# Interleaving two output-projection units, re-cutting the weight slices and splitting the last batch's loads in a fused attention and SwiGLU kernel

## The chip, the cores and the metric

The kernel runs on one core of one Trainium2 chip. The metric is device time in microseconds (us), the median of several executions. The kernel before was put beside every run, so that both are taken on the same chip.

## The reference, cut to what matters

```
# attention with softmaxed features: q over the head dim, k over the sequence
q_s = softmax(q, axis=-1);  k_s = softmax(k, axis=2)          # (8, 8, 576, 64)
kv  = einsum('bhsd,bhse->bhde', k_s, v)
x   = einsum('bhsd,bhde->bhse', q_s, kv)                      # -> 4608 tokens x 512
# SwiGLU block
out = (silu(x @ w_gate) * (x @ w_val)) @ w_out                # 512 -> 1536 -> 512
```

## The kernel before: the parts that matter

Weights are cast to bf16 by DMAs that GpSimd issues. The gate and value weights come in slices of columns, the output weights in four slices of three row blocks. The loads of batch 1 are issued by SyncE when the first output-weight slice has landed.

```python
for c0, n in ((0, 128), (128, 128), (256, 256), (512, 256), (768, 384), (1152, 384)):
    w_slice(wg, moe_w_gate, c0, n)
    w_slice(wv, moe_w_val, c0, n)
w_dma = [wo_slice(m0, 3) for m0 in (0, 3, 6, 9)]
...
after = w_dma[0]
for what, src in (("q", q), ("v", v), ("k", k)):        # batch 1
    ...load(what, src, 1, G, ..., after=after)
```

Batch 0 goes through twelve column blocks (m) of gate and value matmuls. Then come output units 0 and 1 (128 tokens each), and between them and the next ones the attention of batch 1:

```python
for m in range(MT):                       # MT = 12
    m_unit(0, S, m, by_group=(m == 0))    # 8 gate + 8 value matmuls, silu, product
exp_of("q", 1, 0); exp_of("q", 1, 1)      # ScalarE
norm_sum(1, 0); norm_mul(1, 0); norm_sum(1, 1)   # VectorE
o_out(0, o_mm(0), nc.scalar)              # 12 matmuls over the output weights
o_out(1, o_mm(1), nc.scalar)
p2 = o_mm(2, m1=4)
turn_pe(1, 0, 0); turn_pe(1, 0, 1)        # TensorE transposes of VectorE's product
...
i = norm_mul(1, 1)                        # VectorE, second product
cast_v(1, 0)                              # GpSimd
...
o_mm(2, p2, m0=4)
turn_pe(1, 1, 0); turn_pe(1, 1, 1)
...                                       # keys and values, then x of batch 1
chunks = [(S, 448)] + ...                 # "chunk 1" below is the first of these
```

The tail of the program stores the last unit in two parts, each half through SyncE and half through ScalarE (`o_last`).

The softmax here doesn't subtract the row's maximum and nothing guards it: scores larger than these inputs give would overflow.

Of the kernel before, what the change touches and what calls it, by code (L numbers as in the profile page):

```python
# [15 lines left out]
def kernel(  # L16
# [10 lines left out]
    nc = tc.nc  # L27

    B, H, S, D = q.shape
# [3 lines left out]
    MT = d_ff // 128  # L33
    T = S // 64
# [3 lines left out]
    BANKS = ((0, 5), (5, T))  # L38
# [8 lines left out]
    def bank(name):  # L47
        return psp.tile([128, 512], FP32, tag="ps", name=name)
# [16 lines left out]
    def head_ap(src, b, G, t0=0, t1=T):  # L65
        return bass.AP(
            tensor=src.tensor,
            offset=src[b, 4 * G].offset + 64 * t0,
            ap=[[T * 64, 128], [2 * HSTR, 2], [1, (t1 - t0) * 64]],
        )  # L70

    def load(what, src, b, G, pieces=((0, T),), after=None):
        t_ = ld.tile([128, 2, T * 64], FP32, tag=what, name=what)
        raw[what, b, G] = t_
        last = None
        for t0, t1 in pieces:
            last = nc.sync.dma_start(out=t_[:, :, 64 * t0:64 * t1], in_=head_ap(src, b, G, t0, t1))
            if after is not None:
                tc.add_manual_dep(last.ins, after.ins.name, SYNC, reason="order of loads")
                after = None  # L80
        return last

    def load_kv(b):
        for G in range(NG):
            load("k", k, b, G)
            load("v", v, b, G)

    def w_slice(dst, src, c0, n):
        ap = bass.AP(
            tensor=src.tensor,  # L90
            offset=src[0, c0].offset,
            ap=[[d_ff, 128], [128 * d_ff, KT], [1, n]],
        )
        return nc.gpsimd.dma_start(out=dst[:, :, c0:c0 + n], in_=ap)  # L94
# [9 lines left out]
    def copy(eng, out, in_):  # L104
        if eng is nc.scalar:
            nc.scalar.copy(out=out, in_=in_)
        else:
            eng.tensor_copy(out=out, in_=in_)  # L108
# [18 lines left out]
    def norm_sum(b, G, pieces=((0, T),)):  # L127
        s = st[b, G]
        eq2 = s["eq"].rearrange("p t h d -> p (t h) d")
        rs = at.tile([128, 2 * T], FP32, tag="rs", name="rs")  # L130
        first = None
        for t0, t1 in pieces:
            i = nc.vector.reduce_sum(  # L133
                out=rs[:, 2 * t0:2 * t1], in_=eq2[:, 2 * t0:2 * t1, :], axis=mybir.AxisListType.X
            )
            first = first or i
        rr = s["rr"] = at.tile([128, 2 * T], FP32, tag="rr", name="rr")
        nc.vector.reciprocal(out=rr, in_=rs)
        return first
# [152 lines left out]
    def store(j, o_sb, c0=0, c1=512, engs=(nc.sync, nc.sync)):  # L292
        for half in range(2):
            b, t = divmod(2 * j + half, T)
            dst = bass.AP(
                tensor=out.tensor,
                offset=out[b * S + t, c0].offset,
                ap=[[T * d_model, 64], [1, c1 - c0]],
            )
            engs[half].dma_start(out=dst, in_=o_sb[64 * half:64 * half + 64, c0:c1])  # L300

    def o_mm(j, o_ps=None, m0=0, m1=MT):
        if o_ps is None:
            o_ps = bank("o_ps")
        r0 = (j * 128) % RING
        for m in range(m0, m1):
            nc.tensor.matmul(  # L307
                out=o_ps, lhsT=hr[:, m, r0:r0 + 128], rhs=wo[:, m, :],
                start=(m == 0), stop=(m == MT - 1),
            )  # L310
        return o_ps

    def o_out(j, o_ps, eng=nc.vector):
        o_sb = osb.tile([128, 512], FP32, tag="o_sb", name="o_sb")
        copy(eng, o_sb, o_ps)
        store(j, o_sb)
# [20 lines left out]
    with tc.manual_schedule():  # L337
# [23 lines left out]
        norm_mul(0, 0, BANKS)  # L361
        norm_sum(0, 1, BANKS)

        for c0, n in ((0, 128), (128, 128), (256, 256), (512, 256), (768, 384), (1152, 384)):
            w_slice(wg, moe_w_gate, c0, n)
            w_slice(wv, moe_w_val, c0, n)
        w_dma = [wo_slice(m0, 3) for m0 in (0, 3, 6, 9)]
# [88 lines left out]
        norm_sum(1, 0)  # L456
        norm_mul(1, 0)
        norm_sum(1, 1)
        o_out(0, o_mm(0), nc.scalar)
        o_out(1, o_mm(1), nc.scalar)  # L460
        p2 = o_mm(2, m1=4)
        turn_pe(1, 0, 0)
        turn_pe(1, 0, 1)
# [35 lines left out]
        for ci, (c0, n) in enumerate(chunks):  # L499
            b = ci + 2  # L500
# [4 lines left out]
            for m in range(MT):  # L505
# [36 lines left out]
                if m == 8 and more:  # L542
                    for G in range(NG):
                        load("q", q, b + 1, G)
                    if b + 2 < B:
                        load_kv(b + 2)
# [4 lines left out]
        last = n_tok // 128 - 4  # L551
# [33 lines left out]
```

## Time and profile before

| what | value | read in |
|---|---|---|
| time, median of the first 3 runs | 312.39 us | runs |
| time of the one profiled execution | 313.74 us | runs |
| span of that execution | 311.6 us | page |
| TensorE busy / idle | 301.8 / 9.8 us | page, part 1 |
| first gate matmul | 14.21 us | TensorE's timeline |
| first output matmul | 38.76 us | TensorE's timeline |
| chunk 1 starts | 52.65 us | TensorE's timeline |
| last matmul to end of span | 4.09 us | trace |

In a timeline row the columns are start, duration, engine, source line, operation, output and inputs with their shape, the number of instructions merged, and in brackets the idle time before it with what ended it. ScalarE's timeline:

```profile
38.60 1.28 ACT L119 ACT_TABLE_LOAD   x1
40.48 1.16 ACT L119 ACTIVATE eq<-q 128x1152 bf16<-128x1152 f32 x1 [0.60 <-DMA q<-in_q_dram]
```

### The profile page before, as it was taken

How to read it: one execution, taken by the hardware profiler on the slowest of the kernel's cores; microseconds unless marked ns; L12 is line 12 of the kernel's file. 1: busy time of each engine (PE TensorE's matmuls, PEld its weight loads, DVE VectorE, ACT ScalarE, POOL GpSimd, SP SyncE). 2: the span in 40 equal slices, each digit the busy share in tenths (PEclk: the TensorE clock that was granted, in tenths of full speed). 3: DMA queues.
4: the chain of work that ended last, by engine and by line, in shares of the span. 5: the costliest groups of instructions: out<-in, count | busy, mean ns of one | idle time of the engine just before them, and what ended most of it. 6: DMA issues, size and time to landing. Idle time of an engine off the chain costs nothing.

```text
span 311.6 us, 5449 instructions
## 1 busy us (share of the span) xinstructions
PE 301.8 (97%) x2182; PEld 149.2 (48%) x2182; DVE 160.7 (52%) x274; ACT 146.1 (47%) x214; POOL 32.8 (11%) x39
## 2 busy tenths in 40 slices
PE   6899999999999999999999999999999999999994
PEld 2567744555444444444444444444444444444442
DVE  3834477946763567355836492639353334333321
ACT  5843468794764465547364637455143113312300
POOL 2950021510200110002000200000000000000000
PEclk9999999999999999999999999999999999999999
DMA  7999999989356906491729253605310302020034
GB/s 270 188 190 204 274 384 367 364 191 377 107 103 149 374 14 135 91 391 45 143 63 352 109 111 68 187 1 105 68 39 0 69 11 56 2 68 13 21 69 103
DMA packets 41690, 45.78 MB, mean 147 GB/s; under 512 B 18496, under 2 KB 25664, under 8 KB 41664
## 3 DMA queue, kind: packets, MB, share of 16 engines
q1 hardware_dynamic: 32752, 39.99, 43.2%
q0 software_dynamic: 8752, 5.31, 12.0%
q8 instruction: 17, 0.28, 0.4%
q10 hardware_dynamic: 160, 0.13, 0.1%
q14 instruction: 9, 0.07, 0.1%
HBM read 37.75 MB, written 9.44 MB: 151 GB/s over the span
## 4 chain that ended last, share of the span: by engine, by line
PE 85%; DMA 10%; POOL 2%; issue 0%; ACT 0%; SPq 0%; DVE 0%
PE o_ps L307 28%; PE g_ps L282 26%; PE u_ps L282 26%; DMA wo<-in_moe_w_out_dram 6%; DMA wv<-in_moe_w_val_dram 3%; PE kv L187 2%; DMA k<-in_k_dram 2%; PE xp L243 1%; POOL wg L94 1%; PE o_ps L327 1%; POOL wv L94 1%; POOL v L345 0%; PE tp L162 0%; POOL v L342 0%; ACT xt L257 0%
## 5 line engine op out<-in xcount | busy, mean ns | idle before, releaser
L289 ACT ACTIVATE sg<-g_ps 128x512 bf16<-128x512 f32 (+2 forms) x120 | 64.7, 554 | 134.6 <-PE g_ps L282 132.8
L290 DVE TENSOR_TENSOR hr<-sg,u_ps 128x512 bf16<-128x512 bf16 (+2 forms) x120 | 74.2, 630 | 88.3 <-PE u_ps L282 82.6
L282 PE MATMUL g_ps<-xt,wg 128*128 128x512 bf16 (+2 forms) x480 | 111.4, 358 | 0.4 <-DMA wg<-in_moe_w_gate_dram 0.3
L282 PE MATMUL u_ps<-xt,wv 128*128 128x512 bf16 (+2 forms) x480 | 111.3, 358 | 0.2 <-DMA wv<-in_moe_w_val_dram 0.2
L307 PE MATMUL o_ps<-wo,hr 128*128 128x512 bf16 x420 | 94.1, 379 | 0.5 <-DMA wo<-in_moe_w_out_dram 0.5
L282 PEld LDWEIGHTS <-wv 128*128 128x128 bf16 x480 | 46.9, 98 | 46.9 <-DMA wv<-in_moe_w_val_dram 0.5
L282 PEld LDWEIGHTS <-wg 128*128 128x128 bf16 x480 | 46.1, 98 | 46.2 <-DMA wg<-in_moe_w_gate_dram 0.8
L307 PEld LDWEIGHTS <-hr 128*128 128x128 bf16 x420 | 41.0, 98 | 49.3 <-issue 0.8
L108 DVE COPY o_sb<-o_ps 128x512 f32<-128x512 f32 x33 | 22.4, 680 | 39.2 <-PE o_ps L307 39.2
L122 POOL CAST vb<-v 128x1152 bf16<-128x1152 f32 x14 | 17.8, 1276 | 135.3 <-DMA v<-in_v_dram 90.7
L133 DVE TENSOR_REDUCE rs<-eq 128x18 f32<-128x1152 bf16 (+2 forms) x18 | 21.7, 1215 | 13.6 <-ACT eq L119 13.6
L147 DVE TENSOR_TENSOR qs<-eq,rr 128x1152 bf16<-128x1152 bf16 (+2 forms) x18 | 21.7, 1216 | 0.1
L119 ACT ACTIVATE eq<-q 128x1152 bf16<-128x1152 f32 (+2 forms) x18 | 18.3, 1051 | 5.3 <-DMA q<-in_q_dram 5.2
L119 ACT ACTIVATE ek<-k 128x1152 bf16<-128x1152 f32 (+2 forms) x17 | 17.9, 1101 | 0.5 <-DMA k<-in_k_dram 0.5
L289 ACT ACT_TABLE_LOAD x12 | 15.4, 1283 | 0.2
L119 ACT ACT_TABLE_LOAD x11 | 14.1, 1283 | 0.2
L257 ACT CAST xt<-xp 128x512 bf16<-128x512 f32 x14 | 7.8, 587 | 4.3 <-PE xp L243 4.3
L258 DVE CAST xt<-xp 128x512 bf16<-128x512 f32 x14 | 9.0, 683 | 0.7 <-PE xp L243 0.7
L372 PE MATMUL idle<-zero 128*128 128x512 bf16 x20 | 6.3, 465 | 3.0 <-DVE rs L133 1.8
L187 PEld LDWEIGHTS <-ek 64*64 64x64 bf16 x504 | 6.3, 107 | 1.7 <-ACT ek L119 0.4
L187 PE MATMUL kv<-vb,ek 64*64 64x65 bf16 x504 | 6.7, 194 | 0.0
L243 PE MATMUL xp<-qt,kn 64*64 64x512 bf16 (+1 forms) x112 | 6.7, 292 | 0.0
(43 smaller groups left out, 62.2 us busy)
## 6 DMA issues: line engine op xcount, KB each, us to landing
q<-in_q_dram SPq DMA_DIRECT2D x16, 576.0 KB, 8.6
out_dram<-o_sb SPq DMA_DIRECT2D x70, 128.0 KB, 2.3
k<-in_k_dram SPq DMA_DIRECT2D x15, 576.0 KB, 7.5
v<-in_v_dram SPq DMA_DIRECT2D x14, 576.0 KB, 8.7
wo<-in_moe_w_out_dram POOLq DMA_DIRECT2D x4, 384.0 KB, 15.3
wg<-in_moe_w_gate_dram POOLq DMA_DIRECT2D x2, 384.0 KB, 11.4
wv<-in_moe_w_val_dram POOLq DMA_DIRECT2D x2, 384.0 KB, 13.2
wg<-in_moe_w_gate_dram POOLq DMA_DIRECT2D x2, 256.0 KB, 7.7
```

Of the source, the lines that this page charges most:

```text
L108: eng.tensor_copy(out=out, in_=in_)
L119: nc.scalar.activation(out=e[:, t0:t1], in_=src[:, t0:t1], func=AF.Exp)
L122: return nc.gpsimd.tensor_copy(out=vbs[G][:, :, :, 0:64], in_=raw["v", b, G].rearrange("p h (t d) -> p t h d", d=64),)
L133: i = nc.vector.reduce_sum(out=rs[:, 2 * t0:2 * t1], in_=eq2[:, 2 * t0:2 * t1, :], axis=mybir.AxisListType.X)
L147: last = eng.tensor_mul(qs[:, t0:t1, :].rearrange("p t (h d) -> p (t h) d", d=64), eq2[:, 2 * t0:2 * t1, :], s["rr"][:, 2 * t0:2 * t1].to_ ...
L187: nc.tensor.matmul(out=kv[g][HALF[h], c:c + 65], lhsT=ek[HALF[g], t, h, :], rhs=vbs[G][HALF[g], t, h, :], start=(t == 0), stop=(t == T - 1),)
L243: nc.tensor.matmul(out=o[h][HALF[g], c:c + 64 * (t1 - t0)], lhsT=kn[HALF[h], g, G, :], rhs=qt[G][HALF[h], t0:t1, 64 * g:64 * g + 64], star ...
L258: nc.vector.tensor_copy(out=xt[:, 2 * G + 1, c0:c0 + 512], in_=main[G][1])
L282: nc.tensor.matmul(out=gu[a][i][:, 0:w_], lhsT=(wg, wv)[a][:, kk, ms], rhs=xt[:, kk, c:c + w_], start=(kk == 0), stop=(kk == KT - 1),)
L289: nc.scalar.activation(out=sg[:, 0:w_], in_=g_ps[:, 0:w_], func=AF.Silu)
L290: nc.vector.tensor_mul(hr[:, m, r:r + w_], sg[:, 0:w_], u_ps[:, 0:w_])
L307: nc.tensor.matmul(out=o_ps, lhsT=hr[:, m, r0:r0 + 128], rhs=wo[:, m, :], start=(m == 0), stop=(m == MT - 1),)
```

## The change

The intent is plain in the two waits that TensorE's timeline shows. Smaller slices bring the third column block sooner. Interleaving units 0 and 1 asks for the last output-weight slice after 18 matmuls and not after 9. The last batch's loads are cut in pieces: in the first hunk T is 9, and BANKS is the pair of ranges (0, 5) and (5, 9), so that a split load is two transfers.

```diff
     def load_kv(b):
+        whole = ((0, T),)
+        last = b == B - 1
         for G in range(NG):
-            load("k", k, b, G)
-            load("v", v, b, G)
+            load("k", k, b, G, BANKS if last else whole)
+            load("v", v, b, G, BANKS if last and G == 0 else whole)
@@
-        for c0, n in ((0, 128), (128, 128), (256, 256), (512, 256), (768, 384), (1152, 384)):
+        for c0, n in ((0, 128), (128, 128), (256, 128), (384, 256), (640, 384), (1024, 512)):
@@
-        o_out(0, o_mm(0), nc.scalar)
-        o_out(1, o_mm(1), nc.scalar)
+        p = [None, None]
+        for m0 in range(0, MT, 3):
+            for j in range(2):
+                p[j] = o_mm(j, p[j], m0, m0 + 3)
+        for j in range(2):
+            o_out(j, p[j], nc.scalar)
         p2 = o_mm(2, m1=4)
```

## The prediction

> **What bounds the kernel now.** I read the page first, then the list of what TensorE waited for, then the timelines of TensorE, ScalarE and VectorE over the first 55 us, then the landing times of the weight loads, and last the stretches table with the DMA rate. The page's first part says that TensorE is the bound of the whole:
>
> ```profile
> PE 301.8 (97%) x2182; PEld 149.2 (48%) x2182; DVE 160.7 (52%) x274; ACT 146.1 (47%) x214; POOL 32.8 (11%) x39
> ```
>
> Of the span of 311.6 us TensorE is idle for 9.8 us, and the view of its waits says where the named part of that lies:
>
> ```profile
> PE idle L372 <- DVE rs L133: 1.8, 1, 1.8
> PE idle L372 <- DVE sel L351: 1.2, 1, 1.2
> PE kv L395 <- DMA v<-in_v_dram: 0.9, 1, 0.9
> PE o_ps L307 <- DMA wo<-in_moe_w_out_dram: 0.5, 1, 0.5
> PE xp L200 <- DVE kn L408: 0.4, 1, 0.4
> PE g_ps L282 <- DMA wg<-in_moe_w_gate_dram: 0.3, 1, 0.3
> PE u_ps L282 <- DMA wv<-in_moe_w_val_dram: 0.2, 1, 0.2
> ```
>
> Only the three lines that name weights (0.5 + 0.3 + 0.2) can be touched by this change, since the others come before the first gate matmul at 14.2 us. After 53 us the list has no wait: the last 258 us are matmuls end to end. So what can be won or lost lies between 14.2 and 52.7 us, and TensorE's timeline shows the two waits that the change aims at, in brackets:
>
> ```profile
> 18.74 1.15 PE L282 MATMUL g_ps<-xt,wg 128*128 128x320 bf16 x8
> 20.13 1.16 PE L282 MATMUL u_ps<-xt,wv 128*128 128x320 bf16 x8 [0.23 <-DMA wv<-in_moe_w_val_dram]
> ...
> 41.41 0.81 PE L307 MATMUL o_ps<-wo,hr 128*128 128x512 bf16 x3 [0.54 <-DMA wo<-in_moe_w_out_dram]
> ```
>
> The steady step of eight such matmuls is 0.98 us (21.12, 22.10, 23.08 and so on), so the value matmuls of column block m=2 were due at 18.74 + 0.98 = 19.72 and started at 20.13: 0.41 us lost. The second line is output unit 0 at weight row block 9, which waits for the last quarter of the output weights.
>
> The reader should not stop there. Over the same stretch VectorE has a chain of its own (timeline of VectorE):
>
> ```profile
> 41.68 1.35 DVE L133 TENSOR_REDUCE rs<-eq 128x18 f32<-128x1152 bf16 x1 [1.94 <-ACT eq L119]
> 43.06 0.27 DVE L138 RECIPROCAL rr<-rs 128x18 f32<-128x18 f32 x1
> 43.37 1.36 DVE L147 TENSOR_TENSOR qs<-eq,rr 128x1152 bf16<-128x1152 bf16 x1
> 44.64 1.35 DVE L133 TENSOR_REDUCE rs<-eq 128x18 f32<-128x1152 bf16 x1
> 46.02 0.27 DVE L138 RECIPROCAL rr<-rs 128x18 f32<-128x18 f32 x1
> 46.32 1.36 DVE L147 TENSOR_TENSOR qs<-eq,rr 128x1152 bf16<-128x1152 bf16 x1
> ```
>
> It has no gap from 41.68 to 47.68. It starts when ScalarE has exponentiated the queries of batch 1, at 40.48, and ScalarE itself waited 0.60 us there for the load of q. TensorE needs its product at 47.74 for the transposes:
>
> ```profile
> 46.01 1.89 PE L307 MATMUL o_ps<-wo,hr 128*128 128x512 bf16 x8
> 47.74 0.68 PE L162 MATMUL tp<-ident,qs 128*128 128x128 bf16 x9
> ```
>
> 47.68 against 47.74: the two chains meet within 0.06 us. TensorE can't pass this point earlier, whatever it saves before it, unless q lands earlier. And q is issued only when the first output-weight slice has landed (the queue of SyncE waits 30.8 us for it, to 33.56). That slice comes after all gate and value slices in the same queue. So behind TensorE's 97% the stretch from 33.6 to 52.7 us is set by DMA.
>
> **What the Trainium skill says.** (1) "DMA: Bandwidth & Descriptors", section "Why small descriptors are slow (HBM only)": each packet has a fixed overhead, so short runs move fewer bytes per second. A slice of 128 columns is read in runs of 512 B and written, as bf16, in runs of 256 B. The trace agrees, in the stretches table (last number: GB/s of bytes written). The first row is mostly 128-column slices, the second mostly 256 and 384:
>
> ```profile
> 13.00:18.00 5.00, 4.24 (x79) 3.00 (x68) 2.78 (x8) 3.90 (x9) 4.17 (x7) 1.00 1.47 164
> 18.00:33.00 15.00, 14.77 (x120) 11.40 (x119) 5.74 (x14) 5.46 (x16) 3.48 (x5) 1.00 1.32 203
> ```
>
> (2) The same page, section "Issuing engines are not separate DMA queues": all queues end on the same 16 engines. The trace agrees: the last output-weight slice took 18.4 us to land against 14.6, 15.0 and 15.7 of the other three, as q, v and k of batch 1 came in beside it. (3) "Perfetto Trace Analysis", section "DMA Optimizations": splitting may let work start sooner if the DMA engines are generally idle. Here they are not between 2 and 60 us. (4) "TensorE: Matmul & The Clock Gate", section "Wait — 56ns, not 53.3ns?" gives 215.7 ns from start to start for 512 columns; the chain of waits has 24 output matmuls in 5.18 us, 215.8 each. It agrees, and I use the trace's.
>
> **The change part by part.** The count of instructions stays the same on TensorE, VectorE, ScalarE and GpSimd; SyncE gets three load issues more.
>
> *Slices of 3x128, 256, 384, 512 in place of 2x128, 2x256, 2x384.* Bytes and count stay, the sizes change. A 128-column slice is 0.131 MB written. Time by the two rates: before 4 x 0.131/0.164 + (4 x 0.262 + 4 x 0.393)/0.203 = 3.2 + 12.9 = 16.1 us; after 6 x 0.131/0.164 + 2 x (0.262 + 0.393 + 0.524)/0.203 = 4.8 + 11.6 = 16.4 us. So the whole column of weights, and with it q, comes some 0.3 us later. The third value slice landed at 20.05 (issue at 12.35, 7.7 to landing); with half its pair's bytes it comes about 2 x 0.262/0.203 - 2 x 0.131/0.164 = 1.0 us sooner, at 19.1, before it is due at 19.72: the wait of 0.41 goes. But slices get larger and are needed at their first column block. Due times of the value half, 1.96 us per block: m=3 at 21.7, m=5 at 25.6, m=8 at 31.5. Landings: 19.1 + 2.6 = 21.7; + 3.9 = 25.6; and for the last the measured 31.6 (17.66 + 13.9) plus 0.3 = 31.9. Two just on time and the last 0.4 late. Moreover the second-last value slice of before (15.28 + 12.5 = 27.8) landed 3.1 us after its partner, 1.2 more than its bytes need; if such a straggler hits the 384 slice now, m=5 waits 1.1. So 0.41 is taken out and 0.4 to 1.1 put back: a net of 0 to -0.7 us, about nothing. The first output matmul starts at 38.7 to 39.4 (before 38.76).
>
> *Units 0 and 1 interleaved.* The same 24 matmuls; the last slice is wanted after 18 of them and not after 9, 18 x 0.216 = 3.9 us after the start, at 42.6 or later, against a landing at 41.4 (23.00 + 18.4) to 41.7. The wait of 0.54 goes for certain. The evacuations of both units move together to about 44 us on ScalarE, which has 0.78 us idle before the second one: free.
>
> *What becomes of the saved time.* With 24 + 4 matmuls (6.05 us) TensorE reaches the transposes of batch 1 at 44.8 to 45.5. The first product is done at 43.37 + 1.36 = 44.73, plus 0.3 = 45.0. Then 0.5 of transposes and 1.73 of eight matmuls: 47.3 to 47.7; the second product is ready at 47.68 + 0.3 = 48.0. TensorE waits, and goes on at 48.0 where it was 47.74. The saved 0.54 becomes a wait on VectorE, and the later DMA costs about 0.25. From there to 52.65 the steps follow without slack (exponent of k done at 49.26, kv at 49.64, x at 51.56), so this passes to the end.
>
> *Last batch's keys and values in pieces.* Three more issues of about 0.5 us on SyncE at 163.7 to 165.9, with its next store only at 180.3; the exponents of these keys run at 189.0 and still wait for whole tiles. Hidden: 0.
>
> Sum: 0 + 0 + 0.25 + 0 = +0.25 us, from 312.39 to 312.6. As the rate of the small slices in the first row is partly the values' own loads, I take half: 312.5.
>
> **Rivals.** *TensorE gets both waits back* (0.41 + 0.54 = 0.95 us, to 311.4): it needs q to land about 1 us earlier. For it: landing times depend on the slowest of 16 engines, and the straggler of 1.2 us might vanish. Against: bytes and queue order ahead of q are the same. *The 512-column slice stalls* m=8 for over 1 us and exceeds what the later wait on VectorE hides (about 0.6): 313.3. For it: 31.9 against 31.5 is tight, and it is the largest of all; against: the interleaving gives slack behind it. *The pieces disturb the stores or the queue late*: against it, 14 us of idle SyncE after them and no wait of TensorE on a store anywhere.
>
> **Range and chances.** The middle is 312.5. The rivals give 311.4 and 313.3, and the three runs of before spread by 0.95 us by themselves, so 311.6 to 313.3 should hold it 8 times in 10. Two per cent is 6.2 us, while all that the change can reach in idle time is 1 us and no step adds over 2: within 2% is 0.98, the rest shared evenly.
>
> **What would show it.** Right: TensorE's waits lose the output-weight line and the 0.41 at m=2, and gain one at the transposes on the product of VectorE (0.3 to 0.7 us in all), perhaps one on a value slice at m=5 or m=8; the first gate matmul of chunk 1 starts within 0.4 us of 52.65; nothing differs after it. Wrong: q is exponentiated clearly before 40.2, so that TensorE keeps its gain; or a weight wait over 1 us; or a wait after 53 us.

## The result, and the profile after

The changed kernel took 312.58 us (median of 6 runs, 312.19 to 313.03) against 312.27 us before (6 runs, 311.77 to 313.11). The ratio is 1.0011, 95% interval 0.9995 to 1.0028: the same. A ratio here is the mean time of one kernel's fast runs over that of the other's of the same rounds, so it is not quite the ratio of the medians.

The profile, however, says something else. TensorE's timeline of the changed kernel, at the places shown of before:

```profile
18.57 1.14 PE L284 MATMUL g_ps<-xt,wg 128*128 128x320 bf16 x8
19.55 1.14 PE L284 MATMUL u_ps<-xt,wv 128*128 128x320 bf16 x8
...
38.17 6.21 PE L309 MATMUL o_ps<-wo,hr 128*128 128x512 bf16 x27
...
44.72 1.89 PE L309 MATMUL o_ps<-wo,hr 128*128 128x512 bf16 x8
46.57 0.68 PE L164 MATMUL tp<-ident,qs 128*128 128x128 bf16 x9
```

No bracket is left: both waits on weights are gone. The view gives no bracket to an idle time up to 0.15 us, though: from 44.72 to the transposes at 46.57 it is 1.85 us where eight matmuls take 8 x 0.216 = 1.73, so TensorE still waits 0.12 us there for VectorE's product (ready at 45.15 + 1.36 = 46.51, below). Chunk 1 starts at 51.48 us, 1.17 us earlier than in the profile before, and the span is 310.6 us against 311.6. VectorE's second product and ScalarE's exponent moved along:

```profile
45.15 1.36 DVE L149 TENSOR_TENSOR qs<-eq,rr 128x1152 bf16<-128x1152 bf16 x1
```

```profile
38.02 1.28 ACT L121 ACT_TABLE_LOAD   x1
39.31 1.16 ACT L121 ACTIVATE eq<-q 128x1152 bf16<-128x1152 f32 x1
```

Here q was there when the table was (no bracket). Its load had been released at 32.36 us, where it was 33.56 before. A reader of these two profiles alone would write that the change wins 1.2 us. The timed runs say that it wins nothing and may lose 0.3. So either the gain is given back where the profile does not show it, or the two profiles are not of comparable executions.

### The profile page after: what moved, and what is told of

It reads as the page before. It is cut to its first block, busy times and chain, and to the rows that moved or that the text cites. A ratio compares the mean times of both kernels' runs of the same rounds, so it can differ in the third digit from the quotient of the medians.

```text
span 310.6 us, 5430 instructions
## 1 busy us (share of the span) xinstructions
PE 300.3 (97%) x2157; PEld 149.4 (48%) x2182; DVE 160.7 (52%) x274; ACT 146.2 (47%) x214; POOL 32.6 (11%) x39
## 4 chain that ended last, share of the span: by engine, by line
PE 92%; DMA 4%; POOL 1%; issue 1%; ACT 0%; SPq 0%; DVE 0%
PE u_ps L284 30%; PE g_ps L284 30%; PE o_ps L309 29%; DMA wv<-in_moe_w_val_dram 2%; DMA k<-in_k_dram 2%; PE kv L189 2%; PE xp L245 1%; PE o_ps L329 1%; POOL wg L96 0%; POOL v L347 0%; PE tp L164 0%; POOL v L344 0%; POOL wv L96 0%; ACT xt L259 0%; SPq L77 0%
## 5 line engine op out<-in xcount | busy, mean ns | idle before, releaser
L309 PE MATMUL o_ps<-wo,hr 128*128 128x512 bf16 x403 | 92.5, 379 | 1.0 <-issue 0.2
L291 ACT ACT_TABLE_LOAD x12 | 15.4, 1283 | 0.2
L121 ACT ACT_TABLE_LOAD x11 | 14.1, 1283 | 0.2
```

Source lines behind the costliest of these rows:

```text
L121: nc.scalar.activation(out=e[:, t0:t1], in_=src[:, t0:t1], func=AF.Exp)
L291: nc.scalar.activation(out=sg[:, 0:w_], in_=g_ps[:, 0:w_], func=AF.Silu)
L309: nc.tensor.matmul(out=o_ps, lhsT=hr[:, m, r0:r0 + 128], rhs=wo[:, m, :], start=(m == 0), stop=(m == MT - 1),)
```

## The experiments

Twelve runs were made, two of them of unchanged kernels. A table at the end of this section puts the same instants of all profiles side by side. "Excess" is explained with the first experiment.

### The control and the three parts alone

**The kernel before again, unchanged** (no edit).

> The kernel before, unchanged, as a control. In the two profiles the first output-weight slice landed at 33.6 us (before) and 32.4 us (after), and chunk 1 began at 52.65 and 51.48 us, though the timed runs show no gain (312.27 against 312.58). Theory A (the profiled run of before was a late one: a straggling value slice, not the kernel): this profile shows the first output-weight slice landing nearer 32.4, chunk 1 beginning at 51.3 to 52.0 and a span near 310. Theory B (the changed slices really bring the weights 1.2 us earlier and something later takes it back): again 33.5 and 52.6. Time ratio 1.000 within 0.0015 in both.

Measured: 312.25 us, ratio 0.9994 (0.9977 to 1.0010). Its profile (execution of 312.32 us, so a typical one) has no wait on weights at all. TensorE's list of waits, without two of the warm-up at the start:

```profile
...
PE kv L395 <- DMA v<-in_v_dram: 0.7, 1, 0.7
PE xp L200 <- DVE kn L408: 0.4, 1, 0.4
```

and the timelines of TensorE, VectorE and ScalarE:

```profile
38.12 6.21 PE L307 MATMUL o_ps<-wo,hr 128*128 128x512 bf16 x28
...
44.67 1.89 PE L307 MATMUL o_ps<-wo,hr 128*128 128x512 bf16 x8
46.51 0.68 PE L162 MATMUL tp<-ident,qs 128*128 128x128 bf16 x9
```

```profile
45.09 1.36 DVE L147 TENSOR_TENSOR qs<-eq,rr 128x1152 bf16<-128x1152 bf16 x1
```

```profile
37.23 0.71 ACT L289 ACTIVATE sg<-g_ps 128x320 bf16<-128x320 f32 x2 [1.25 <-PE g_ps L282]
37.96 1.28 ACT L119 ACT_TABLE_LOAD   x1
39.26 2.22 ACT L119 ACTIVATE eq<-q 128x1152 bf16<-128x1152 f32 x2
```

The first output-weight slice landed at 31.3 us and the last at 39.3, not at 33.6 and 41.4. The old profile was of a late execution. In it, the second gate slice landed at 16.6 (control: 15.5) and the fifth value slice at 27.8 (control: 25.5), and everything queued behind them was late. Both waits that the change removes belong to that execution. In the control the last slice lands 0.76 us before unit 0 wants it (38.12 + 9 x 0.216 = 40.06).

The control also gives the floor of the stretch. From the first output matmul to chunk 1 it takes 51.42 - 38.12 = 13.30 us, with one short wait in it. TensorE is through its eight matmuls at 44.67 + 8 x 0.216 = 46.40, VectorE's second product is ready at 45.09 + 1.36 = 46.45, and the transposes start at 46.51. So VectorE's chain ends last there, by 0.1 us. That chain starts at ScalarE: last silu, table load, exponent, none of them waiting for a load. (The silu waits for TensorE's last gate matmuls, so the whole stretch moves with TensorE.) "Excess" in the table is what a profile has above 13.30 us.

**The interleaving alone** (third hunk of the diff).

> The interleaving alone. Theory A (behind TensorE's waits the chain q load, exponent, sum, product on VectorE sets when the transposes of batch 1 can start): the wait on the last output-weight slice is gone, TensorE waits at the transposes of batch 1 instead, time 312.3, ratio 1.000 within 0.0015. Rival C (the interleaving wins its 0.5 us and another part of the change gives it back): 311.8, ratio 0.998.

Measured: 312.47 us, ratio 0.9999 (0.9980 to 1.0018), so theory A's number and not rival C's. TensorE waits at both transposes, 0.56 and 0.55 us, as theory A said, but only in part because of q. Its profile is of the slowest of its six executions (313.66 us), with an excess of 1.33 us, and there is a new cause in it. Of the excess, 0.45 is q coming late. The rest is VectorE's first product, which took 2.25 us. Here are VectorE and GpSimd of this kernel:

```profile
42.46 2.25 DVE L147 TENSOR_TENSOR qs<-eq,rr 128x1152 bf16<-128x1152 bf16 x1
```

```profile
42.36 1.14 POOL L122 CAST vb<-v 128x1152 bf16<-128x1152 f32 x1 [19.30 <-DMA v<-in_v_dram]
```

and of the control:

```profile
42.14 1.36 DVE L147 TENSOR_TENSOR qs<-eq,rr 128x1152 bf16<-128x1152 bf16 x1
```

```profile
42.68 1.82 POOL L122 CAST vb<-v 128x1152 bf16<-128x1152 f32 x1 [20.01 <-DMA v<-in_v_dram]
```

Whoever starts first runs at its own speed, and the other stretches: the product from 1.36 to 2.25, or the cast from about 1.15 to 1.82. The Trainium skill says so ("SBUF — State Buffer", section "Who interferes with whom"): a VectorE instruction with two SBUF inputs and a GpSimd instruction that reads SBUF share one read port, the first holds it for its whole length, and the second blocks. The traces agree in all 14 profiles. In two (this one, and e10_one_more with 2.23 us) the cast of v began about 0.1 us before the product and VectorE lost 0.9. In the other twelve the product was first. In the profiles it goes by when v happens to land; none ties it to a part of the change.

**The slices alone** (second hunk).

> The slices of 3x128, 256, 384 and 512 alone. Theory A: the wait of 0.4 us on the third value slice is gone, q lands 0 to 0.3 us later, time 312.3 to 312.6. Rival C: 312.9, ratio 1.002. Theory B: q lands over 1 us earlier than in the control and chunk 1 begins over 1 us earlier.

Measured: 312.35 us, ratio 1.0000 (0.9981 to 1.0019). No wait on any weight. The first output-weight slice landed at 31.3 us, exactly as in the control, so theory B (the slices bring the weights earlier) falls. Chunk 1 began 0.55 us earlier than in the control (50.87), but so did the first gate matmul (14.03 against 14.59). Theory A's "q lands 0 to 0.3 us later" was not met: q landed at 38.59, in the control at 38.74. Excess 0.01.

**The pieces alone** (first hunk).

> Only the last batch's keys and values in pieces. All theories of the early stretch: no change before 160 us, three more load issues of some 0.5 us each on SyncE, time 312.3, ratio 1.000 within 0.0015. A ratio over 1.001 would say that the pieces are what costs 0.3 us.

Measured: 312.73 us, ratio 1.0010 (0.9994 to 1.0026). This is the largest of the four medians, and "no change" is not what the profile shows either. All steps from chunk 1 to the last matmul are equal to the control's within 0.02 us, but the span ends 4.31 us after the last matmul and not 3.93. What was found of the cause is at the end of this section.

### Moving the moment at which q is released

The prediction rests on q's landing. These runs move it.

**The changed kernel again** (no edit).

> The changed kernel again, for a second profile and more timed runs. Theory A (the landing of the first output-weight slice varies from run to run by about 1 us, in both kernels): that slice lands anywhere from 32.4 to 33.6 and chunk 1 begins 19.1 us after it as in the first profile (32.4 and 51.5); time 312.2 to 312.8. Theory B (the change brings the weights 1.2 us earlier each time): 32.4 and 51.5 again.

Measured: 312.79 us, ratio 1.0005 (0.9983 to 1.0026). The first output-weight slice landed at 32.1 us and the excess was 0. Chunk 1 came 19.5 us after that landing and not 19.1, as theory A had it: the landing does not set it. The second gate slice, which the change does not re-cut, was late (16.7 us) and TensorE waited for it at column block m=1, with 0.38 us in brackets: this wait the change doesn't take away. Between this, the first profile and the controls, landings of 31.3 to 33.6 were seen with no order by kernel.

**The changed kernel, q, v and k of batch 1 released by the last value slice:**

```diff
-            w_slice(wv, moe_w_val, c0, n)
+            wv_dma = w_slice(wv, moe_w_val, c0, n)
...
-        after = w_dma[0]
+        after = wv_dma
```

> The changed kernel, but the loads of batch 1 are released by the last value slice and not by the first output-weight slice (about 2 us earlier). Theory A (q's landing sets the end of the early stretch): q is exponentiated 0.5 to 2 us earlier, chunk 1 begins 0.5 to 1.5 us earlier, time 311 to 311.8. Rival D (TensorE's own work and the output weights set it): output weights land later as q takes their place, a wait on them comes back, time 312.5 or more.

Measured: 312.96 us, ratio 1.0017 (0.9995 to 1.0040). The loads went out at 29.27 us and q was exponentiated 1.14 us after the first output matmul (38.54 against 37.40), just as in the control (39.26 against 38.12). Nothing came earlier by this clock, because ScalarE had to finish its silu and load its table:

```profile
38.54 2.33 ACT L121 ACTIVATE eq<-q 128x1152 bf16<-128x1152 f32 x2
```

There is no bracket: q was waiting for ScalarE. So theory A, that q's landing sets the end of this stretch, falls for a typical execution. (That the silu and the table load are the head of the chain is read from the timelines; no run moved them.) A wait of 0.28 us on the output weights came back, as rival D said, and it is the excess of 0.32.

**The kernel before with the same earlier release** (same edit on the kernel before).

> The kernel before with the same earlier release. Here unit 0 needs the last output-weight slice after 9 matmuls. Theory A plus the reading that interleaving is a tolerance for late output weights: the wait on the output weights grows from 0.5 to 1 to 2.5 us and eats what q's earlier landing gives, so the time is 0.3 to 1 us above that of the changed kernel with the earlier release. Rival D: the same wait grows and the time is above 312.8.

Measured: 314.35 us, ratio 1.0060 (1.0042 to 1.0078), the only run clearly apart. The last output-weight slice landed at 41.9 us in it and at 41.7 in the run before, but the waits differ. From the lists of the two kernels, this one and then the changed one:

```profile
PE o_ps L307 <- DMA wo<-in_moe_w_out_dram: 2.1, 1, 2.1
```

```profile
PE o_ps L309 <- DMA wo<-in_moe_w_out_dram: 0.3, 1, 0.3
```

The interleaving does what it was made for: with the weights equally late it turns a wait of 2.11 us into 0.28, worth 314.35 - 312.96 = 1.4 us of time (I had expected 0.3 to 1). These two kernels also differ in slices and pieces, but the wait is on the output weights in both and only the interleaving changes when those are wanted.

**The changed kernel, loads released by the second output-weight slice:** `after = w_dma[1]`.

> The changed kernel with the loads of batch 1 released by the second output-weight slice (about 1.8 us later). Theory A: everything from the transposes of batch 1 on is later, TensorE waits there 1 to 2 us, time 313 to 314.3. Rival D: there is slack, time 312.6 within 0.3.

Measured: 312.61 us, ratio 1.0012 (0.9989 to 1.0035). ScalarE waited 0.36 us for q and the excess is 0.35: q's lateness goes through one to one when there is any. But it was 0.36 and not 1 to 2, since q took 5.4 us from issue to landing (33.48 to 38.85) where it took 7.4 in the control, presumably with less left in front of it. The size in my expectation was wrong; rival D's "slack" is nearer.

### The end of the span

**The change without the pieces** (first hunk undone).

> The interleaving and the slices, without the pieces. The profiles so far split by one thing after the last matmul: the five kernels with pieces end 4.15 to 4.35 us after it, the five without 3.95 to 4.11. Theory P (the pieces cost some 0.24 us at the end and nothing else of the change costs anything): tail 4.0, distance from the first output matmul to chunk 1 again 13.3, time 312.3. If the 0.3 us of the change came from the early stretch: tail 4.0 and time 312.6.

Measured: 312.41 us, ratio 1.0004 (0.9985 to 1.0022), last matmul to end 3.99 us. q was 0.21 us late and the excess is 0.20. This is the version that the experiments point to, and it does not beat the kernel before.

Twelve profiles, e12_batch6 below among them, split cleanly. The six with the three extra loads end 4.17 to 4.34 us after the last matmul (mean 4.27); the six without end 3.93 to 4.09 (mean 3.99). (The expectation above has slightly other figures, from spans rounded to 0.1 us.) The instants that differ are those of the last stores. VectorE's last copies and the stores of the control, in the views of the timeline and of the store line from 306.0 us (durations in ns, first and last start in us):

```profile
305.62 0.96 DVE L331 COPY o_sb<-o_ps 128x384 f32<-128x384 f32 x2 [1.26 <-PE o_ps L327]
```

```profile
L300 SPq DMA_DIRECT2D out_dram<-o_sb x2: 466/492/519, 306.2 to 306.8; - x2
L300 ACTq DMA_DIRECT2D out_dram<-o_sb x2: 557/640/722, 306.2 to 306.9; - x2
```

and of the kernel with the pieces alone:

```profile
305.39 0.96 DVE L333 COPY o_sb<-o_ps 128x384 f32<-128x384 f32 x2 [1.26 <-PE o_ps L329]
```

```profile
L302 SPq DMA_DIRECT2D out_dram<-o_sb x2: 467/467/467, 306.0 to 306.9; - x2
L302 ACTq DMA_DIRECT2D out_dram<-o_sb x2: 552/642/732, 306.0 to 306.6; - x2
```

In the control SyncE issues its last store 0.21 us after the last copy (306.79 against 305.62 + 0.96), ahead of ScalarE. With the pieces it does so 0.51 us after (306.86 against 306.35), behind ScalarE. The offset is 0.21 us in all six profiles without and 0.51 to 0.52 in all six with. The span, however, ends after the last landing, and that is ScalarE's store in all of them: 2.45 us after the copy in the control, 3.01 with the pieces. ScalarE issued it at the same offset (0.27 to 0.29 us in all 14 profiles), but it took 2.74 us to land and not 2.17. So SyncE's late store and ScalarE's slow one go together; what links them is not shown. The next three runs ask what the three extra loads, which landed over 100 us earlier, have to do with it.

**One split load and not three:** `load("k", k, b, G)` in place of the split keys.

> The changed kernel with only one split load (the last batch's first values), so one load issue more than before and not three. The completion semaphores of the loads and stores are taken in turn from eight, so each extra issue moves the last four stores by one place. Theory L (it is that place that costs): a tail different from both, anywhere from 4.0 to 4.3. Theory N (each issue more costs): 4.1.

Measured: 312.35 us, ratio 0.9995 (0.9972 to 1.0017). Last matmul to end 3.88 us, the shortest of all; SyncE's last store at 0.20 us. Theory N (each issue costs) said 4.1, so it falls; 3.88 is also below theory L's 4.0 to 4.3.

**Eight more issues:** `last = b >= B - 2`, all keys and values of two batches split.

> The changed kernel with all keys and values of the last two batches split: eight load issues more than before, so the last four stores have the same semaphores as before. Theory L (place in the turn of eight): tail 4.0 again, time 312.3. Theory N (the number of issues): tail 4.3 or more, time 312.7 or more.

Measured: 312.16 us, ratio 1.0003 (0.9975 to 1.0031). SyncE's last store is back at 0.18 us and the last landing at 2.42 us after the copy, as theory L (the place in the turn of eight semaphores) has it. But the span ended 4.39 us after the last matmul, against L's 4.0 and within N's "4.3 or more" (N's time of 312.7 or more was not met). The excess lies after the last landing: a wait of the final handshake of the engines was 1.0 us here and 0.5 in the control. So L is right on the stores and not on the end, and one profile doesn't tell why.

**The three split loads in the batch before:** `last = b == B - 2`.

> The three split loads moved from the last batch to the one before it: three issues more, but not in the last batch. Theories L and N: tail 4.15 to 4.35 as in the changed kernel. If something of the last batch's own data made the tail longer: 4.0.

Measured: 312.57 us, ratio 1.0004 (0.9984 to 1.0024). Last matmul to end 4.34 us, store at 0.51: as with the pieces in the last batch. So it is not that batch's data.

What is shown: with three more issues on SyncE its last store is 0.3 us later, in whichever batch they are, while with one and with eight more (one profile each) it is not. The place in the turn can be read in the packed traces, which keep the number of the semaphore that each transfer updates. SyncE and ScalarE use eight in turn: 101, 104 to 106 and 115 to 118. The last four stores have 104, 105, 106 and 115 with no and with eight more issues, 105, 106, 115 and 116 with one, 115 to 118 with three. None of these stores had to wait for the last user of its semaphore, which had landed 4.7 to 7.4 us earlier wherever the traces have the landing. So the place differs as theory L says; why these places should be slow stays open.

### All profiles side by side

| kernel | first output matmul | first output weights landed | chunk 1 | excess over 13.30 | its cause in the profile | last matmul to end | us of this execution |
|---|---|---|---|---|---|---|---|
| before, first profile | 38.76 | 33.6 | 52.65 | 0.59 | output weights 0.54, q 0.60, side by side | 4.09 | 313.74 |
| after, first profile | 38.17 | 32.3 | 51.48 | 0.01 | | 4.28 | 312.87 |
| e1_before | 38.12 | 31.3 | 51.42 | 0.00 | | 3.93 | 312.32 |
| e2_interleave | 38.00 | 31.7 | 52.63 | 1.33 | q 0.45, shared port 0.88 | 4.02 | 313.66 |
| e3_slices | 37.56 | 31.3 | 50.87 | 0.01 | | 3.96 | 311.82 |
| e4_pieces | 37.88 | 31.4 | 51.19 | 0.01 | | 4.31 | 312.62 |
| e5_after | 38.30 | 32.1 | 51.60 | 0.00 | | 4.20 | 312.93 |
| e6_after_gate_wv | 37.40 | 31.2 | 51.02 | 0.32 | output weights 0.28 | 4.30 | 312.43 |
| e7_before_gate_wv | 37.70 | 31.4 | 53.15 | 2.15 | output weights 2.11 | 3.97 | 314.11 |
| e8_after_gate_wo1 | 37.39 | 31.6 | 51.04 | 0.35 | q 0.36 | 4.17 | 312.37 |
| e9_no_pieces | 38.04 | 32.4 | 51.54 | 0.20 | q 0.21 | 3.99 | 312.50 |
| e10_one_more | 37.91 | 31.4 | 52.08 | 0.87 | shared port 0.87 | 3.88 | 313.10 |
| e11_eight_more | 37.46 | 31.5 | 50.77 | 0.01 | | 4.39 | 311.77 |
| e12_batch6 | 38.00 | 31.4 | 51.30 | 0.00 | | 4.34 | 312.90 |

Two things are to be read here. The excess is 0 whenever nothing comes late in this stretch, with and without each part of the change, and otherwise it is the wait named to within 0.05 us. And much of what makes the slow executions (313.1 to 313.7) slow is chance of landing: 1.33 and 0.87 us here in e2_interleave and e10_one_more, and 0.59 in the first profile of before, which had lost another 1.0 before this stretch. There, from the first gate to the first output matmul, it took 24.55 us, the control 23.53. The first gate matmul itself wanders between 13.8 and 14.6 us from run to run.

## Why the prediction was right, and where its steps were not

**The time.** I said 312.5 us with 0.98 on "within 2%"; it is 312.58, ratio 1.0011. The class was safe, with 1 us of idle time in reach. That the number fits to 0.1 us is in part luck: the sum of +0.25 is made of steps that did not happen as told (below), and the small loss it forecast is not clear of the noise. By the prediction's own signs the first profile after the change says "wrong": q was exponentiated at 39.31, clearly before 40.2, and chunk 1 began at 51.48, not within 0.4 of 52.65. Of the signs of "right", the two weight waits did go, but the transposes wait 0.12 us for VectorE and not 0.3 to 0.7.

**"The two chains meet within 0.06 us; TensorE can't pass this point earlier."** Right, and the step that carries the result. In the control they meet again: TensorE is free at 46.40, the product ready at 46.45, and the stretch is 13.30 us in every undisturbed profile, interleaved or not. That they met in the late profile as well was luck: there the weights had held TensorE up by 0.71 us (41.41 against 38.76 + 9 x 0.216 = 40.70) and q had held VectorE's chain up by 0.60.

**"Unless q lands earlier", and "the stretch is set by DMA".** Wrong for a typical execution. Released 2.1 us earlier than in the control (29.27 against 31.34), q brought nothing; the head of the chain is ScalarE's last silu and table load. Only when q is late does it count, one to one (0.21, 0.36). The profile I read was one of the late ones.

**"The wait of 0.54 goes for certain", and the 0.41 at m=2.** They do go, but in the control neither exists in the kernel before. What was for sale was not 1 us spent behind a second chain; in a typical run it was 0.

**"0.4 to 1.1 put back at m=5 or m=8."** Measured 0: no profile with the new slices waits there. I took the landing of the last value slice from the late profile (31.6 plus 0.3); with the new slices alone it landed at 29.4, before it is due.

**"q comes some 0.3 us later."** Mis-sized. In the control the 128-column slices landed 0.73 us apart and the 256-column ones 1.3 to 1.4, so I estimate from these intervals that a third small pair costs about 2 x 0.73 - 1.34 = 0.1 us, and no profile shows the first output weights later by more than they vary anyway.

**"Hidden: 0", of the pieces.** Wrong by the 0.27 us that the six and six profiles show after the last matmul (4.27 against 3.99). I looked for an effect where the loads are (163 to 189 us) and there is none; it was at the last stores. In time it is not clear of noise: the four runs that have the pieces and the usual release (first result, e4, e5, e12) average 312.70 us over 22 runs, and the four without (e1, e2, e3, e9) 312.46 over 24, on chips that were not the same for all. Their ratios, each taken beside the kernel before on the same chip, have means of 1.0008 and 0.9999, which is 0.25 us; but a single ratio is known to about 0.002 only. It is nevertheless the only part of the change with a cost that repeats.

**The rivals.** "TensorE gets both waits back" is what the two first profiles look like and what the control refutes. The stall of the 512-column slice never came. The late disturbance by the pieces, which I ruled out by the idle SyncE queue, is the one that has something to it.

**The check that was to be had before predicting.** The profiled execution of before took 313.74 us, while its timed runs had a median of 312.39 and a maximum of 313.11. A trace from the slow end can show waits that the median does not have, as this one did.

## What to carry to other kernels

Before pricing a wait of under 1 us, compare the profiled execution's own time with the median, and look at a second profile: a wait that is only in the slow one is worth its frequency, not its length; here 7 of the 45 timed executions of the kernel before, and 2 of the 12 of the changed one, took over 313.0 us. When two engines' chains meet within 0.1 us, taking a wait out of one buys tolerance, not time; here the interleaving held 0.28 us against 2.11 when the weights were made late. After adding issues to a queue, look at that queue's last store as well as at the new transfers.

## What the Trainium skill lacked or had wrong

- "ScalarE: Activation LUTs", section "What ACT_TABLE_LOAD costs", adds a drain of about 1380 ns to the load's 1283 ns for each switch of set. The load is 1283 ns here too, but no such drain shows: in the control silu ends at 37.94, the load runs from 37.96 to 39.24, and the exponent starts at 39.26. A switch costs 1.3 us.
- No page that I read says how much a queue of weight loads varies between executions of one kernel: the first output-weight slice landed between 31.2 and 33.6 us in 14 profiles.
- No page that I read has the late last store: with three more issues earlier in SyncE's queue its last store went out 0.51 to 0.52 us after its data were ready, against 0.18 to 0.21 with none, one or eight more, and the last landing came 2.88 to 3.04 us after the data, against 2.42 to 2.58.
